# Expert products of a mixture-of-experts kernel, by whole blocks and by 2x2 blocks with seven block products

## The chip, the cores and the metric

The kernel runs on one core of a Trainium2 chip. A core has a matrix engine (TensorE, PE in the profile; its weight loads are listed as PEld), a vector engine (VectorE, DVE), a scalar engine (ScalarE, ACT), a programmable engine (GpSimd, POOL) and a sequencer that mostly issues transfers (SyncE, SP). They share an on-chip memory of 128 partitions, SBUF; TensorE writes its results to a second one, PSUM, in eight banks of 512 float32 values per partition. Each engine works through its own list of instructions in order and waits for others on semaphores. The metric is the time of the launch on the device, in microseconds, as the median of several runs; the profile shows one further execution.

## The reference

Two parts run one after the other: causal attention with a window of 64, and a layer of eight experts, of which each token uses the one with the largest router logit.

```python
# attention: q, k, v of shape (8, 8, 576, 64), window 64, softmax, times v -> x of shape (4608, 512)
logits = x @ w_gate                       # (4608, 8)
expert_idx = np.argmax(logits, axis=1)
gate_w = softmax(logits)[arange, expert_idx]
for e in range(8):                        # over the tokens of each expert
    h = np.maximum(x_sorted[lo:hi] @ w1[e], 0.0)     # 512 -> 1024
    y_sorted[lo:hi] = h @ w2[e]                      # 1024 -> 512
out = gate_w[:, None] * y
```

Everything is float32. The inputs come from a fixed seed, so the number of tokens per expert is fixed: 669, 400, 748, 505, 592, 390, 566 and 738.

## The kernel before

The kernel has three stages. The first (lines 100 to 350) computes the attention in 96 small steps that are interleaved by hand, stores the rows of x in DRAM (`x_dram`) and collects the router's logits. It also loads expert 0's weights (lines 334 to 336) into the first of the weight buffers, `ws[0]`.

The second stage (lines 353 to 479), some 40 us, routes. The tokens of each expert are laid out in slots, in tiles of TB = 128 slots that belong to one expert each; an expert's last tile is padded. VectorE computes each token's slot, and 36 matmuls with one-hot matrices (lines 473 to 477) turn that around into `perm_i`, the token in each slot, and `gate_s`, its gate. Also computed are `tile_e` (the expert of each tile), `load_i` (whether a tile must load weights: whether its expert differs from that of the tile NW before it, which used the same buffer) and `used_i` (how many tiles there are). The sizes of these operations depend on NS (slot columns), NTILE (the most tiles there can be, 43) and NCUT (the fewest, 36).

The third stage (lines 482 to 560) works through the tiles, and it is this that the change rewrites. For each tile:

- `fetch(i)` reads the expert and the load flag into registers of SP, issues the two conditional weight loads of 2 MB (w1 and w2) into buffer i % 3 on SP's queue, and has GpSimd gather the tile's 128 rows of x (`indirect_dma_start`, line 503). It runs two tiles ahead.
- `turn(i)` transposes the rows in four 128x128 blocks on TensorE (line 511); VectorE copies them to SBUF (line 512).
- `work(i)` makes the first layer in 32 matmuls, weights stationary, 128 slots streaming (line 523). In the profile a float32 matmul shows as two passes, so these are 64 entries. VectorE clears the negative values of the first half of h (line 530), ScalarE those of the second (line 528). Then comes `turn(i + 1)`, and the second layer in 8 matmuls (16 passes) with blocks of h stationary and 512 columns of w2 streaming (line 535). ScalarE multiplies by the gate (line 539), and GpSimd scatters the rows to the output (line 541).

The framework's scheduler orders each engine's list by readiness and by the order of the program, except for SP, whose order is the program's (line 489). The first 36 tiles are straight code; the rest are in pairs under `tc.If(used > i0)` (lines 555 to 560), and nothing is moved across the border of an If. With the given tokens 40 tiles are used.

Of the kernel before, what the change touches and what calls it, by code (L numbers as in the profile page):

```python
# [10 lines left out]
F32 = mybir.dt.float32  # L11
BF16 = mybir.dt.bfloat16
I32 = mybir.dt.int32
AF = mybir.ActivationFunctionType
ALU = mybir.AluOpType
AX = mybir.AxisListType
PSUM = bass.MemoryType.PSUM
# [18 lines left out]
def kernel(  # L36
# [10 lines left out]
    nc = tc.nc  # L47
    P = nc.NUM_PARTITIONS
    B, H, S, D = q.shape
    NT, DM = out.shape  # L50
    E = moe_w_gate.shape[1]
    FF = moe_w1.shape[2]
    scale = 1.0 / math.sqrt(D)

    NG = H // 2
# [5 lines left out]
    NTB = BG * S // P  # L61
    NJ = NT // P
    FT = FF // P
    TB = P
    NTILE = (NT + TB - 1) // TB + E - 1
    NS = NTILE
    NW = 3
    NCUT = (NT + TB - 1) // TB
    assert D == WINDOW and 2 * D == P and NG * P == DM and NB * WINDOW == S
    assert S - SM == WINDOW and KB == NV + 1 and NTB * P == BG * S and B % BG == 0 and NTILE * TB <= 128 * P  # L70
# [5 lines left out]
    x_dram = dram.tile([NT + 1, DM], F32, name="x_dram")  # L76
# [402 lines left out]
        V.tensor_copy(out=gate_s[:], in_=slots[:, 1, :])  # L479


    with (
        tc.tile_pool(name="wp", bufs=1) as wp,
        tc.tile_pool(name="mp", bufs=2) as mp,
        tc.tile_pool(name="xgp", bufs=1) as xgp,
        tc.tile_pool(name="ps_xt", bufs=2, space=PSUM) as ps_xt,
        tc.tile_pool(name="ps_h", bufs=4, space=PSUM) as ps_h,
        tc.tile_pool(name="ps_y", bufs=2, space=PSUM) as ps_y,
        tc.manual_schedule(engines={mybir.EngineType.SP}),
    ):  # L490
        HF = FT // 2
        NX = 4
        ws += [weights(wp, i) for i in range(1, NW)]
        xgs = [xgp.tile([P, DM], F32, name=f"xg{i}") for i in range(NX)]
        xgTs = [xgp.tile([P, NG, TB], F32, name=f"xgT{i}") for i in range(2)]

        def fetch(i):
            w1, w2 = ws[i % NW]
            e = nc.sync.value_load(tile_e[0:1, i : i + 1], min_val=0, max_val=E - 1)
            new = nc.sync.value_load(load_i[0:1, i : i + 1], min_val=0, max_val=1)  # L500
            nc.sync.dma_start(out=w1[:], in_=w1v[:, bass.ds(e, 1), :, :], cond=new, cond_hint=False)
            nc.sync.dma_start(out=w2[:], in_=w2v[:, bass.ds(e, 1), :, :], cond=new, cond_hint=False)
            nc.gpsimd.indirect_dma_start(  # L503
                out=xgs[i % NX][:], out_offset=None, in_=x_dram[:, :],
                in_offset=bass.IndirectOffsetOnAxis(ap=perm_i[:, i : i + 1], axis=0),
            )

        def turn(i):
            tp = ps_xt.tile([P, NG, P], F32, name="tp")
            for g in range(NG):  # L510
                nc.tensor.transpose(out=tp[:, g, :], in_=xgs[i % NX][:, g * P : (g + 1) * P], identity=ident[:])  # L511
            nc.vector.tensor_copy(out=xgTs[i % 2][:], in_=tp[:])  # L512

        def work(i, ahead):
            w1, w2 = ws[i % NW]
            xgT = xgTs[i % 2]
            hT = mp.tile([P, FT, TB], F32, name="hT")
            for m in range(2):
                hp = ps_h.tile([P, HF, TB], F32, name="hp")
                for f in range(HF):  # L520
                    for g in range(NG):
                        c0 = (m * HF + f) * P
                        nc.tensor.matmul(  # L523
                            hp[:, f, :], lhsT=w1[:, 0, g, c0 : c0 + P], rhs=xgT[:, g, :],
                            start=(g == 0), stop=(g == NG - 1),
                        )
                if m:
                    nc.scalar.activation(out=hT[:, m * HF :, :], in_=hp[:], func=AF.Relu)  # L528
                else:
                    nc.vector.tensor_scalar_max(hT[:, 0:HF, :], hp[:], 0.0)  # L530
            if ahead:
                turn(i + 1)
            yp = ps_y.tile([P, DM], F32, name="yp")
            for f in range(FT):
                nc.tensor.matmul(  # L535
                    yp[:], lhsT=hT[:, f, :], rhs=w2[:, 0, f, :], start=(f == 0), stop=(f == FT - 1),
                )
            y = mp.tile([P, DM], F32, name="y", bufs=4)
            nc.scalar.activation(out=y[:], in_=yp[:], func=AF.Copy, scale=gate_s[:, i : i + 1])  # L539

            nc.gpsimd.indirect_dma_start(  # L541
                out=out[:, :], out_offset=bass.IndirectOffsetOnAxis(ap=perm_i[:, i : i + 1], axis=0),
                in_=y[:], in_offset=None, bounds_check=NT - 1, oob_is_err=False,
            )

        AHEAD = NW - 1
        for i in range(AHEAD):
            fetch(i)
        turn(0)
        for i in range(NCUT):  # L550
            fetch(i + AHEAD)
            work(i, True)

        used = nc.values_load(used_i[0:1, 0:1], min_val=NCUT, max_val=NTILE)
        for i0 in range(NCUT, NTILE, 2):
            with tc.If(used > i0):
                for i in range(i0, min(i0 + 2, NTILE)):
                    if i + AHEAD < NTILE:
                        fetch(i + AHEAD)
                    work(i, i + 1 < NTILE)  # L560


# [26 lines left out]
```

## Time and profile before

| what | before |
|---|---|
| median of 3 runs | 901.77 us (900.93 to 903.26) |
| the profiled execution | 907.11 us, span 905.4 us |
| attention and its start | 0 to about 263 us |
| routing | to about 302 us |
| expert stage | 302 to 892 us, then 13 us to the end of the span |
| TensorE busy in the span | 843.1 us (93%) |
| VectorE, ScalarE, GpSimd busy | 231.6, 181.7, 124.6 us |
| weight-load issues on SP | 86, of 2 MB each, of which the flag lets some through |
| 2 KB-row gathers and scatters | 42 and 40, each about 1.0 us of GpSimd |

The profile lists the work by groups: the source line, the engine, the operation, the tiles it writes and reads, the shape and number of instances, then their busy time and mean duration, and after the bar how long the engine had stood idle before them and what ended that. Matmuls are pipelined, so their mean duration is longer than the distance from one to the next, and the distance is what costs. A view in order of time has the start, the length and the work. A view by stretches has the busy time of each engine in a window, the clock granted to TensorE as a share of its full one, and the share of the transfer engines that was in use. An arrow names what ended a wait.

### The profile page before, as it was taken

What the parts mean: (1) busy time and instruction counts of PE and PEld (TensorE: products, weight loads), DVE (VectorE), ACT (ScalarE), POOL (GpSimd) and SP (SyncE); (2) the same over time, 40 slices, a digit from 0 to 9 for tenths busy, and PEclk for the clock granted to TensorE, in tenths of its full rate; (3) what the DMA queues carried; (4) which work ended last, traced back from release to release, by engine and by line L of the source; (5) the groups of instructions that cost most, each with busy time, mean ns of one, the idle gap of its engine ahead of it and who ended that gap; (6) DMA issues with size and microseconds to landing.
All of it is one profiled execution on the core that took longest, in us unless ns stands there. A gap on an engine that the chain in (4) does not pass through costs nothing. (4 is left out here: it accounts for less than half of the span.)

```text
span 905.4 us, 16347 instructions
## 1 busy us (share of the span) xinstructions
PE 843.1 (93%) x6668; PEld 617.7 (68%) x6668; DVE 231.6 (26%) x500; ACT 181.7 (20%) x486; POOL 124.6 (14%) x177
## 2 busy tenths in 40 slices
PE   7997999998953699999999999999999999999993
PEld 5775776776733577686767777686777768677772
DVE  4664665664655000000101000010101001010100
ACT  4553554553510000001000000010000001000000
POOL 3111111011000201111111111111111111101010
PEclk9998999998985599999999999999999999999998
DMA  6668677886020661793951494891794871880110
GB/s 139 150 163 200 142 190 193 212 221 160 3 105 0 235 230 36 280 320 144 315 212 47 148 347 165 308 315 39 240 321 156 314 256 36 316 294 23 36 47 11
DMA packets 164863, 159.99 MB, mean 177 GB/s; under 512 B 118320, under 2 KB 118320, under 8 KB 164786
## 3 DMA queue, kind: packets, MB, share of 16 engines
q1 hardware_dynamic: 153362, 129.01, 45.8%
q0 software_dynamic: 6560, 20.45, 6.2%
q10 hardware_dynamic: 4864, 9.44, 3.1%
q8 instruction: 55, 0.90, 0.4%
q14 instruction: 22, 0.18, 0.1%
HBM read 219.69 MB, written 19.92 MB: 265 GB/s over the span
## 5 line engine op out<-in xcount | busy, mean ns | idle before, releaser
L523 PEld LDWEIGHTS hp<-xgT,w 128*128 128x128 f32 x2560 | 294.1, 193 | 18.8 <-issue 18.7
L523 PE MATMUL hp<-xgT,w 128*128 128x128 f32 x2560 | 294.4, 276 | 0.0
L535 PE MATMUL yp<-w,hT 128*128 128x512 f32 x640 | 281.3, 592 | 0.0
L535 PEld LDWEIGHTS yp<-w,hT 128*128 128x128 f32 x640 | 118.5, 190 | 133.9 <-issue 133.9
L530 DVE TENSOR_SCALAR hT<-hp 128x512 f32<-128x512 f32 x40 | 27.7, 692 | 390.9 <-PE hp L523 390.9
L237 ACT ACTIVATE pr<-sc,mx 128x128 f32<-128x128 f32 x288 | 79.4, 375 | 71.9 <-DVE mx L234 53.3
L528 ACT ACTIVATE hT<-hp 128x512 f32<-128x512 f32 x40 | 23.9, 597 | 310.2 <-PE hp L523 310.2
L541 POOL DMA_INDIRECT out_dram<-y,perm_i x40 | 40.6, 1016 | 316.7 <-ACT y L539 303.2
L539 ACT ACTIVATE y<-yp,gate_s 128x512 f32<-128x512 f32 x40 | 27.5, 687 | 266.1 <-PE yp L535 266.1
L503 POOL DMA_INDIRECT xg<-x_dram,perm_i x42 | 41.0, 975 | 235.6 <-PE tp L511 179.2
L512 DVE COPY xgT<-tp 128x512 f32<-128x512 f32 x41 | 28.3, 691 | 137.2 <-PE tp L511 137.2
L234 DVE TENSOR_REDUCE mx<-sc 128x3 f32<-128x384 f32 x96 | 49.1, 553 | 42.5 <-PE sc L227 41.1
L246 PE MATMUL tr<-ident,pr 128*128 128x128 f32 x288 | 49.5, 287 | 0.1
L246 PEld LDWEIGHTS tr<-ident,pr 128*128 128x128 f32 x288 | 34.7, 146 | 20.1 <-ACT qT L190 7.7
L227 PE MATMUL sc<-kT,qT 64*64 64x128 f32 x1152 | 47.7, 289 | 0.1
L227 PEld LDWEIGHTS sc<-kT,qT 64*64 64x64 f32 x1152 | 34.3, 139 | 13.0 <-issue 8.3
L261 PE MATMUL px<-va,pT 128*64 128x65 f32 x640 | 43.1, 231 | 0.0
L168 POOL COPY vb<-va 64x520 f32<-64x520 f32 x32 | 19.7, 617 | 158.5 <-DMA va<-in_v_dram 144.4
L261 PE MATMUL px<-vb,pT 128*64 128x65 f32 x512 | 41.4, 229 | 0.0
L307 PE MATMUL lg<-xT,wg 128*32 128x384 f32 x96 | 39.9, 498 | 0.7 <-DVE xT L287 0.7
L261 PEld LDWEIGHTS px<-vb,pT 128*64 128x64 f32 x512 | 33.4, 141 | 8.8 <-DVE xT L287 4.0
L261 PEld LDWEIGHTS px<-va,pT 128*64 128x64 f32 x640 | 36.3, 138 | 2.9 <-issue 2.8
(93 smaller groups left out, 476.6 us busy)
## 6 DMA issues: line engine op xcount, KB each, us to landing
w<-in_moe_w_dram SPq DMA_DIRECT2D x86, 2048.0 KB
qs<-in_q_dram SPq DMA_DIRECT2D x64, 128.0 KB
ks<-in_k_dram SPq DMA_DIRECT2D x64, 128.0 KB
va<-in_v_dram SPq DMA_DIRECT2D x64, 128.0 KB
x_dram<-xs ACTq DMA_DIRECT2D x8, 1024.0 KB
qs<-in_q_dram SPq DMA_DIRECT2D x32, 32.0 KB
ks<-in_k_dram SPq DMA_DIRECT2D x32, 32.0 KB
vb<-in_v_dram SPq DMA_DIRECT2D x32, 32.0 KB
```

Of the source, the lines that this page charges most:

```text
L227: nc.tensor.matmul(out_, lhsT=qT[rows, t, a * WINDOW : (a + 1) * WINDOW], rhs=rhs, start=False, stop=True, skip_group_check=True,)
L234: nc.vector.tensor_reduce(out=mx[:], in_=scs[h][:], axis=AX.X, op=ALU.max, negate=True)
L237: nc.scalar.activation(out=pr[:, m, :], in_=scs[h][:, m, :], func=AF.Exp, bias=mx[:, m : m + 1])
L246: nc.tensor.transpose(out=tr[:, m, :], in_=prs[h][:, m, :], identity=ident[:])
L261: nc.tensor.matmul(px[a * D : (a + 1) * D, h, m, :], lhsT=pTs[h][:, m, a * D : (a + 1) * D], rhs=vt[:, h, :], start=True, stop=True, skip_ ...
L307: nc.tensor.matmul(lgs[bg][c * WC : (c + 1) * WC, :], lhsT=wg[:, g, :], rhs=xTs[u][:, c, :], start=(g == 0), stop=(g == NG - 1), skip_grou ...
L503: nc.gpsimd.indirect_dma_start(out=xgs[i % NX][:], out_offset=None, in_=x_dram[:, :], in_offset=bass.IndirectOffsetOnAxis(ap=perm_i[:, i : ...
L512: nc.vector.tensor_copy(out=xgTs[i % 2][:], in_=tp[:])
L523: nc.tensor.matmul(hp[:, f, :], lhsT=w1[:, 0, g, c0 : c0 + P], rhs=xgT[:, g, :], start=(g == 0), stop=(g == NG - 1),)
L530: nc.vector.tensor_scalar_max(hT[:, 0:HF, :], hp[:], 0.0)
L535: nc.tensor.matmul(yp[:], lhsT=hT[:, f, :], rhs=w2[:, 0, f, :], start=(f == 0), stop=(f == FT - 1),)
L541: nc.gpsimd.indirect_dma_start(out=out[:, :], out_offset=bass.IndirectOffsetOnAxis(ap=perm_i[:, i : i + 1], axis=0), in_=y[:], in_offset=N ...
```

## The change

Tiles hold 256 slots, as two halves of 128. There are two weight buffers for three. Each layer's product is cut in 2x2 blocks: the first layer's weights in halves of the 512 inputs and halves of the 1024 outputs, with the tile's two halves of slots; the second layer's product in the two halves of slots, halves of 1024 and halves of 512. Seven products of blocks replace eight, in the form of Strassen's method by Winograd, with sums of blocks made beforehand and results combined afterwards.

- Sums of weight blocks: `sums_w1` on GpSimd, four of 1024 elements per partition for each tile; `sums_w2` on VectorE, the same size.
- Sums of the transposed tokens: four of 256 on GpSimd, after ScalarE has copied the transposes to SBUF.
- Sums of the hidden blocks: four of 512 on VectorE.
- First layer (`hidden`): seven products of eight 128x128x128 matmuls each. Two products add into one PSUM bank where the method wants their sum, with another product between them while ScalarE or VectorE reads the first. VectorE makes five combinations, ScalarE a copy and four ReLUs.
- Second layer (`output`): seven products of four matmuls with 256 streaming columns. The gates are applied as the products leave PSUM, three times on ScalarE and five times, with an addition, on VectorE. Two scatters follow.
- Order (`step`): the first layer of tile i, the transposes of tile i+1, then the second layer of tile i-1. Gathers run two tiles ahead, w1 two tiles, w2 one.
- After 18 tiles of straight code each further step is inside an If that holds the next one; the Else of each holds the second layer of the tile before it. 25 tiles are the most there can be.

```diff
-    TB = P
+    TB = 2 * P
+    C = TB // P
-    NS = NTILE
-    NW = 3
+    NS = NTILE * C
+    NW = 2
...
+        xgs = [[mp.tile([P, DM], F32, name=f"xg{i}_{c}") for c in range(C)] for i in range(2)]
+        xq = mp.tile([P, 2, 2, HG, P], F32, name="xq")
+        xs = mp.tile([P, 4, HG, P], F32, name="xs")
+        hqs = [mp.tile([P, 2, 2, HF, P], F32, name=f"hq{i}") for i in range(2)]
+        hs = mp.tile([P, 4, HF, P], F32, name="hs")
...
+        tps = [ps_xt.tile([P, NG, P], F32, name=f"tp{i}") for i in range(2)]
+        hps = [ps_h.tile([P, HF, P], F32, name=f"hp{i}") for i in range(3)]
+        yps = [ps_y.tile([P, HM], F32, name=f"yp{i}") for i in range(3)]
+        def left_sums(eng, s, a11, a12, a21, a22):
+            eng.tensor_tensor(out=s[:, 0], in0=a21, in1=a22, op=ALU.add)
+            eng.tensor_tensor(out=s[:, 1], in0=s[:, 0], in1=a11, op=ALU.subtract)
+            eng.tensor_tensor(out=s[:, 2], in0=a11, in1=a21, op=ALU.subtract)
+            eng.tensor_tensor(out=s[:, 3], in0=a12, in1=s[:, 1], op=ALU.subtract)
+        def right_sums(eng, t, b11, b12, b21, b22):
+            eng.tensor_tensor(out=t[:, 0], in0=b12, in1=b11, op=ALU.subtract)
+            eng.tensor_tensor(out=t[:, 1], in0=b22, in1=t[:, 0], op=ALU.subtract)
+            eng.tensor_tensor(out=t[:, 2], in0=b22, in1=b12, op=ALU.subtract)
+            eng.tensor_tensor(out=t[:, 3], in0=t[:, 1], in1=b21, op=ALU.subtract)
...
         def turn(i):
+            for c in range(C):
+                tp = tps[c]
+                for g in range(NG):
+                    nc.tensor.transpose(
+                        out=tp[:, g, :], in_=xgs[i % 2][c][:, g * P : (g + 1) * P], identity=ident[:]
+                    )
+                nc.scalar.copy(out=xq[:, :, c], in_=tp[:].rearrange("p (a g) s -> p a g s", a=2))
+            right_sums(nc.gpsimd, xs, xq[:, 0, 0], xq[:, 0, 1], xq[:, 1, 0], xq[:, 1, 1])
...
+        def hidden(i):
+            a11, a12, a21, a22 = w1q(i)
+            s, hq = sums[i % NW][0], hqs[i % 2]
+            def product(acc, a, b, first=True):
+                for f in range(HF):
+                    for g in range(HG):
                         nc.tensor.matmul(
+                            acc[:, f, :], lhsT=a[:, g, f * P : (f + 1) * P], rhs=b[:, g, :],
+                            start=(first and f == 0 and g == 0), stop=(g == HG - 1), skip_group_check=True,
                         )
+            relu = partial(nc.scalar.activation, func=AF.Relu)
+            p1, u2, u3 = part
+            x, y = bank(hps, 0), bank(hps, 0)
+            product(x, a11, xq[:, 0, 0])
+            nc.scalar.copy(out=p1[:], in_=x[:])
+            product(y, s[:, 1], xs[:, 1])
+            V.tensor_tensor(out=u2[:], in0=y[:], in1=p1[:], op=ALU.add)
+            product(x, a12, xq[:, 1, 0], False)
+            relu(out=hq[:, 0, 0], in_=x[:])
+            product(y, s[:, 2], xs[:, 2], False)
+            V.tensor_tensor(out=u3[:], in0=y[:], in1=p1[:], op=ALU.add)
+            z, w = bank(hps, 0), bank(hps, 0)
+            product(z, s[:, 0], xs[:, 0])
+            V.tensor_tensor(out=hq[:, 1, 1], in0=z[:], in1=u3[:], op=ALU.add)
+            relu(out=hq[:, 1, 1], in_=hq[:, 1, 1])
+            product(w, a22, xs[:, 3])
+            V.tensor_tensor(out=hq[:, 1, 0], in0=u3[:], in1=w[:], op=ALU.subtract)
+            relu(out=hq[:, 1, 0], in_=hq[:, 1, 0])
+            product(z, s[:, 3], xq[:, 1, 1], False)
+            V.tensor_tensor(out=hq[:, 0, 1], in0=z[:], in1=u2[:], op=ALU.add)
+            relu(out=hq[:, 0, 1], in_=hq[:, 0, 1])
+        def output(i):
+            b11, b12, b21, b22 = w2q(i)
+            t, hq, y2 = sums[i % NW][1], hqs[i % 2], ys[i % 2]
+            a11, a12, a21, a22 = hq[:, 0, 0], hq[:, 1, 0], hq[:, 0, 1], hq[:, 1, 1]
+            left_sums(V, hs, a11, a12, a21, a22)
...
+            product(x, a11, b11)
+            scaled(out=p1a[:], in_=x[:], scale=gates[0])
+            scaled(out=p1b[:], in_=x[:], scale=gates[1])
+            product(y, hs[:, 1], t[:, 1])
+            onto(u2[:], y[:], 0, p1a[:])
+            product(x, a12, b21, False)
+            scaled(out=y2[0][:, lo], in_=x[:], scale=gates[0])
+            product(y, hs[:, 2], t[:, 2], False)
+            onto(u3[:], y[:], 1, p1b[:])
+            z, w = bank(yps, 1), bank(yps, 1)
+            product(z, hs[:, 0], t[:, 0])
+            onto(y2[1][:, hi], z[:], 1, u3[:])
+            product(w, a22, t[:, 3])
...
+            product(z, hs[:, 3], b22, False)
+            onto(y2[0][:, hi], z[:], 0, u2[:])
...
+        def sums_w1(i):
+            left_sums(nc.gpsimd, sums[i % NW][0], *w1q(i))
+        def sums_w2(i):
+            right_sums(V, sums[i % NW][1], *w2q(i))
+        def step(i):
+            hidden(i)
+            if i + 1 < NTILE:
                 turn(i + 1)
+            if i + 2 < NTILE:
+                gather(i + 2)
+                load_w(i + 2, 0)
+            if i + 1 < NTILE:
+                sums_w1(i + 1)
+            if i:
+                output(i - 1)
+                if i + 1 < NTILE:
+                    load_w(i + 1, 1)
+            sums_w2(i)
+        gather(0)
+        load_w(0, 0)
+        load_w(0, 1)
+        gather(1)
+        load_w(1, 0)
+        load_w(1, 1)
+        sums_w1(0)
+        turn(0)
         for i in range(NCUT):
+            step(i)
...
+            with tc.If(used > i) as there:
+                step(i)
+                more(i + 1)
+            taken[:] = was
+            with there.Else():
+                output(i - 1)
+        more(NCUT)
```

## The prediction, made before the result was known

> **What bounds the kernel now.** I read the page's groups first, then busy time by stretches, then the order of time of two tiles late in the expert stage, then the start of that stage. The profiled execution took 907.11 us (span 905.4 and 1.7 around it); the median is 901.77, so it runs 5.3 us long, and my differences are carried over to the median.
>
> Busy time in stretches (stretch, its length, then PE, weight load, VectorE, ScalarE, GpSimd, granted clock, DMA share, GB/s):
>
> ```profile
> 271.00:312.00 41.00, 17.65 (x81) 16.98 (x81) 15.04 (x25) 0.00 (x0) 4.62 (x5) 0.50 0.23 84
> 312.00:892.00 580.00, 579.76 (x3357) 426.35 (x3356) 55.32 (x80) 50.88 (x80) 75.97 (x77) 1.00 0.56 196
> ```
>
> In the expert stage TensorE is never free: 579.8 of 580 us at full clock, the others at 10 to 13%. Whatever shortens TensorE's list there shortens the kernel, until another engine is late. One tile in order of time (start, length, what):
>
> ```profile
> 841.38 7.03 PE L535 MATMUL yp<-w,hT 128*128 128x512 f32 x16
> ...
> 848.25 7.31 PE L523 MATMUL hp<-xgT,w 128*128 128x128 f32 x64
> 848.25 7.11 PEld L523 LDWEIGHTS hp<-xgT,w 128*128 128x128 f32 x63 [0.24 <-issue]
> ...
> 855.39 0.60 PE L511 MATMUL tp<-ident,xg 128*128 128x128 f32 x4
> ...
> 855.83 7.03 PE L535 MATMUL yp<-w,hT 128*128 128x512 f32 x16
> ```
>
> Starts are what counts: the second layer holds TensorE for 848.25-841.38 = 6.87 us (429 ns per 512 columns), the first for 855.39-848.25 = 7.14 (111.6 ns per 128), the transposes 0.44 (110 each): 14.45 us a tile. Weight loads run at the same 111.6 ns and hide. The 40 tiles make 578 us.
>
> The groups that price the new work (instances, total, mean ns):
>
> ```profile
> L530 DVE TENSOR_SCALAR hT<-hp 128x512 f32<-128x512 f32 x40 | 27.7, 692 | 390.9 <-PE hp L523 390.9
> L528 ACT ACTIVATE hT<-hp 128x512 f32<-128x512 f32 x40 | 23.9, 597 | 310.2 <-PE hp L523 310.2
> L539 ACT ACTIVATE y<-yp,gate_s 128x512 f32<-128x512 f32 x40 | 27.5, 687 | 266.1 <-PE yp L535 266.1
> L168 POOL COPY vb<-va 64x520 f32<-64x520 f32 x32 | 19.7, 617 | 158.5 <-DMA va<-in_v_dram 144.4
> L270 DVE TENSOR_TENSOR xs<-px,rec 128x384 f32<-128x384 f32 x48 | 26.7, 556 | 1.4
> L172 POOL COPY vb<-va 64x390 f32<-64x390 f32 x32 | 16.2, 507 | 22.3 <-DMA va<-in_v_dram 11.9 <-PE sc L227 8.7
> L471 DVE TENSOR_TENSOR hi<-hi,tok_m 128x1548 f32<-128x1548 f32 x1 | 1.8, 1772 | 0.0
> L397 DVE TENSOR_TENSOR oh<-logits,r_mx 128x288 f32<-128x288 f32 x1 | 0.5, 460 | 0.0
> ```
>
> The start of the stage, in order of time: gathers are issued one per 1.26 us, and the first lands some 7 us later.
>
> ```profile
> 302.22 1.14 POOL L503 DMA_INDIRECT xg<-x_dram,perm_i  x1 [42.28 <-DVE gate_s L479]
> ...
> 306.18 0.95 POOL L503 DMA_INDIRECT xg<-x_dram,perm_i  x1 [0.30 <-issue]
> ...
> 311.93 9.41 PE L523 MATMUL hp<-xgT,w 128*128 128x128 f32 x64
> ```
>
> **How many tiles.** The reference's seeded inputs send 669, 400, 748, 505, 592, 390, 566 and 738 tokens to the eight experts. In tiles of 128 that is 6+4+6+4+5+4+5+6 = 40, as the x40 says; in tiles of 256 it is 3+2+3+2+3+2+3+3 = 21, which hold 42 old ones. Padding eats 5% of the 12.5% that seven products for eight save.
>
> **TensorE per new tile.** First layer: 7 products of 8 matmuls in two passes, 112 x 111.6 ns = 12.50 us. Second: 7 of 4 in two passes over 256 columns, a width that no row has. Between 128 (111.6) and 512 (429) lies 217.5 on the line; half the 512 is 214.6, twice the 128 is 223.2. I take the line, as both rows lie on it: 56 x 217.5 = 12.18. Transposes 8 x 0.11 = 0.88. Sum 25.56; 21 tiles 536.8 against 578: **-41.2 us** (-44.6 to -34.5). The one transpose group of a tile that is never used exists in both.
>
> **VectorE per tile.** From L397 and L471 an operation on two SBUF inputs costs 0.16 us + 1.04 ns an element: four weight sums of 1024 at 1.22 = 4.9, four sums of hidden blocks of 512 at 0.69 = 2.8. Five combinations of 512 out of PSUM at 0.69 (L530, L270) = 3.5, five of 256 at 0.42 = 2.1. Together 13.3 of 25.6 us. **ScalarE:** two transposed copies, one copy of a product and four ReLUs make seven passes of 512 at 0.60 (L528) = 4.2, three scalings of 256 lie between L237's 375 ns for 128 and L539's 687 for 512, 0.48 each: 5.6. Both fit beside TensorE.
>
> **GpSimd per tile.** Four sums of 1024 and four of 256 on two inputs, two gathers, two scatters. No row has a two-input operation of GpSimd. L168 and L172 give a copy 0.18 us + 0.85 ns an element: 1.04 us for 1024, 0.39 for 256. Lower end: a second input is free; upper end: it costs a second copy, 2.09 and 0.79. I take the upper, since two streams must be read. 4 x 2.09 + 4 x 0.79 + 4 x 1.0 (L503, L541) = 15.5 us, at least 9.7; both under 25.6. A scatter queued behind a sum goes up to 2.09 late, and its buffer is wanted again only two tiles on. The Trainium skill, "GPSIMD Engine Reference", Performance versus the Vector engine, gives 4497 ns for a two-input add of 2048, 2.2 ns an element; by it GpSimd would have an estimated 16.7 us a tile, the same verdict.
>
> **The waits inside a tile.** TensorE now comes back to a PSUM bank that another engine must have read, with one other product between: 1.79 us in the first layer, 1.74 in the second. The handover costs about 0.26 us (the first half ends at 848.25+3.57 = 851.82, VectorE starts at 852.08), the release 0.14 (in the attention stage a VectorE copy ends at 225.73 and the waiting weight load starts at 225.87). So the first layer's two waits for VectorE have 1.79-0.26-0.69-0.14 = 0.70 us to spare, the second's two 0.92, those for ScalarE 0.44 or more (two scalings of 0.48 in 1.74). They hold only while VectorE is free: a weight sum of 1.22 just begun eats 0.5 too much. Queued behind a late combination on VectorE are the next combinations and the hidden sums, which only the following tile's output needs. With VectorE's other work at 7.7 of 25.6 us, four waits x 0.3 chance x about 0.25 = 0.3 us a tile, **+6.3** in all (0 to +15). The interleaving hides the rest: a hidden block has a whole layer (12 us) until its product, the transposed tokens pass ScalarE and GpSimd (about 5 us) while the other tile's output holds TensorE.
>
> **The head.** GpSimd is in order: gathers until 307.1, four sums of expert 0's weights until 315.5, then two token sums until 317.1. The first product starts as before at 311.9 and, at the slow start's 147 ns (9.41/64), ends at 314.3; the second waits until 317.2: +2.9 (0 if a sum costs 1.04; +8.4 if the scheduler puts the weight sums ahead of the gathers, which wait for the slot table). Tile 0 has no output between its first layer and tile 1's: copies and two token sums show, +1.0. Three routing operations grow from 1548 to 1800 elements (+0.26 each), four shrink (-0.15 each): +0.2. Slot matmuls of 100 for 86 columns are held by their 128-column load. Sum **+4.1** (0.2 to 9.6).
>
> **The tail.** Two scatters follow the last combination for one: +1.0. The last output lies in an Else block: VectorE sums its hidden blocks only after the previous output's last combination, 0.26+0.42+1.38+0.14 = 2.2 against 1.74 of cover: +0.5. The jump: existing Ifs show no gap on TensorE, so 0 at best; if each engine must fetch its code, I bound it by the fastest DMA landing in the trace, 3.4. I take 2. Sum **+3.5** (1 to 5).
>
> **DMA.** Weight loads fall from 23 pairs to 15 (a change of expert reloads two buffers, not three). SP's list stays in order of need: layer 1's load of tile i+2 waits for first layer i, then layer 2's of i+1 for output i-1. A 2 MB half at the page's best slice, 348 GB/s, takes 6 us and has over 20 before its sums. Nothing; it would cost only if slower than 100 GB/s.
>
> **Sum.** 907.1-41.2+6.3+4.1+3.5 = 879.8 profiled; minus 5.3 is **874.5, say 875**. Own range 860 to 893.
>
> **Rivals.** (1) *VectorE and GpSimd block each other*, slower. Nothing in the trace shows both on SBUF sums together: GpSimd's rows in the expert stage are DMA issues alone, so a loss of 0 is as open as a whole one. If a VectorE sum must wait out a GpSimd sum of 2.09, its eight fillers grow from 7.7 to some 16 us, and a combination behind one can come up to 2.09+1.22-0.7 = 2.6 late. Four waits x 0.63 x about 1.0 = 2.5 us a tile, 53 in all in place of 6.3: 921. It decides above (27.3+6.3)/21 = 1.6 us a tile. The Trainium skill speaks against the change here: "SBUF — State Buffer", Who interferes with whom, says a VectorE instruction with two SBUF inputs contends with a GpSimd instruction that reads SBUF, and that the second to issue "fully blocks". By it the sum is an estimated 921, without it 875; no run here shows it yet. Against it: list scheduling can place the sums away from the waits, as gathers are already issued tiles early.
> (2) *GpSimd becomes the bound*: needs 25.6-5.4 us over 5120 elements, 3.9 ns an element, 4.7 times its copy. At 28 us a tile: +50, 925.
> (3) *Every product start costs an issue gap.* The attention stage shows 0.17 us of "issue" before loads that had waited; here 14 starts x 0.17 x 21 = +50, 918. Against it: three hand-offs a tile show none today. At the four tight waits alone it is +14, 889.
>
> **How the numbers follow.** My case 0.60, (1) 0.24, (2) 0.06, (3) 0.10. The measurement can tell about 0.3% (2.7 us). Faster: nearly all of mine, a fifth of (1), half of (3): 0.66; same 0.05; slower 0.29. The range to hold it 8 times in 10 runs from 860 to 922, into the middle of (1).
>
> **What would show it.** Right: x2352 first-layer and x1176 second-layer matmuls, starts 111.6 and about 217 apart, a tile every 26 us, TensorE 98% busy. Wrong: VectorE sums well above 0.69 and 1.22 or GpSimd's above 2.1 while the other runs (1); GpSimd without idle (2); TensorE holes of 0.17 at each product (3). My forecast falls if 256 columns cost over 230 ns or a tile loses over 1.6 us.

## The result and the profile after

The changed kernel takes 1053.36 us (median of 4 runs, 1042.62 to 1061.36) against 902.51 (900.93 to 905.41) for the kernel before on the same chip. Two of the changed kernel's runs, 1058.53 and 1061.36, were in a slower state, so the ratio and all differences below take the other two, 1045.4 us in the mean. That is 1.158 times as long, with an interval of 1.150 to 1.165. The prediction of 875 us, faster, was wrong in sign, and the time lies far above its range. Two things make up the loss, and either alone is enough for a kernel slower than before: VectorE's list was put in an order in which it stands waiting for a weight load with TensorE's next work queued behind it, and VectorE's sums were held up by GpSimd's. With both taken away the same seven products run in 861.82 us, 0.953 times the time before.

The profiled execution took 1042.62 us (span 1040.9). Busy time by stretches of the expert stage, with the same columns as before (start and end, length, then PE, weight load, VectorE, ScalarE, GpSimd, granted clock, DMA share, GB/s):

```profile
306.00:1028.00 722.00, 580.62 (x3695) 542.95 (x3693) 327.76 (x375) 112.56 (x211) 383.39 (x256) 0.90 0.32 111
```

Before, TensorE was busy for 579.8 of 580 us at clock 1.00. Now it stands idle for 722.0-580.6 = 141 us, and its busy time has not come down to the 537 us that the prediction worked out, because the mean granted clock is 0.90. Here is what ended TensorE's waits in that stretch (waiting line, releasing line, total us, times, longest):

```profile
PE hp L573 <- DVE part L584: 118.6, 16, 9.4
PE yp L609 <- DVE y L617: 9.4, 4, 2.9
PE hp L573 <- POOL xs L523: 6.8, 2, 3.5
PE hp L573 <- DVE hq L591: 3.7, 3, 1.2
```

One wait makes 118.6 of the 141 us. Line 584 is the first layer's first combination (`u2 = y + p1`); until VectorE has read that bank, the product of block a12's sum cannot be added into it. VectorE itself takes 0.69 us for it, so the question is what VectorE does before. One tile in order of time, first TensorE:

```profile
629.09 1.95 PE L573 MATMUL hp<-xq,w 128*128 128x128 f32 x16
630.88 1.95 PE L573 MATMUL hp<-xs,s 128*128 128x128 f32 x16
632.66 1.95 PE L573 MATMUL hp<-xq,w 128*128 128x128 f32 x16
642.40 6.59 PE L573 MATMUL hp<-xs,s 128*128 128x128 f32 x32 [7.79 <-DVE part L584]
648.83 1.95 PE L573 MATMUL hp<-xs,w 128*128 128x128 f32 x16
```

and then VectorE:

```profile
629.69 0.68 DVE L518 TENSOR_TENSOR hs<-hq,hs 128x512 f32<-128x512 f32 x1
639.39 1.23 DVE L522 TENSOR_TENSOR s<-w 128x1024 f32<-128x1024 f32 x1 [9.01 <-DMA w<-in_moe_w_dram]
640.53 1.22 DVE L524 TENSOR_TENSOR s<-w 128x1024 f32<-128x1024 f32 x1
641.66 0.69 DVE L584 TENSOR_TENSOR part<-hp,part 128x512 f32<-128x512 f32 x1
```

The product that line 584 reads ends at 632.7. By then the first sum of the w2 blocks (line 522) is ahead of it in VectorE's list. In the program these sums stand at the end of a step, behind all combinations; the scheduler moved two of them forward. Their weights are loaded into a buffer that the output just ahead of this first layer frees (there are two buffers, so it is the output of the tile two before), and SP issues that load at 629.28, when the output ends (this row merges two issues, and the first one is meant):

```profile
629.28 21.70 SPq L538 DMA_DIRECT2D w<-in_moe_w_dram  x2
```

So VectorE stands idle for 9.01 us, makes two sums, and reads the bank 9 us late. The load takes 639.39-629.28 = 10.1 us from issue to first use; in the 14 waits of this kind behind the stage's first one it is 9.5 to 10.7.

The hole has a second price. The two products after it need 648.83-642.40 = 6.43 us for 32 passes, where products without a hole before them start 1.78 us apart, so that 32 passes take 3.57. The granted clock is 1.00 from 629.1 to 632.6, 0.50 from 642.4 to 645.6, and 1.00 again from 648.8. Behind the 15 holes of 6.4 to 9.4 us in the first layer the next 32 passes take 5.0 to 6.5 us, some 33 us more in all; that is most of the 44 us by which TensorE is busy for longer than the 537 of the prediction.

The groups show the rest (instances, total, mean ns):

```profile
L522 DVE TENSOR_TENSOR s<-w 128x1024 f32<-128x1024 f32 x21 | 36.3, 1731 | 132.3 <-DMA w<-in_moe_w_dram 132.3
L515 POOL TENSOR_TENSOR s<-w 128x1024 f32<-128x1024 f32 x22 | 52.1, 2368 | 228.1 <-DMA w<-in_moe_w_dram 191.3
L517 POOL TENSOR_TENSOR s<-w 128x1024 f32<-128x1024 f32 x22 | 56.6, 2572 | 0.0
```

VectorE's sum waited 132.3 us for its weights, GpSimd's 191.3 for its own, which delays only GpSimd. And VectorE's sum takes 1731 ns in the mean where the one above took 1.23 us. What holds it shows elsewhere in order of time:

```profile
839.44 5.37 DVE L517 TENSOR_TENSOR hs<-hq 128x512 f32<-128x512 f32 x1
839.60 2.35 POOL L517 TENSOR_TENSOR s<-w 128x1024 f32<-128x1024 f32 x1
841.91 2.34 POOL L518 TENSOR_TENSOR s<-w,s 128x1024 f32<-128x1024 f32 x1
844.73 0.47 DVE L617 SCALAR_TENSOR_TENSOR y<-yp,gate_s,party 128x256 f32<-128x256 f32 x1
845.25 2.91 PE L609 MATMUL yp<-w,hs 128*128 128x256 f32 x8 [2.87 <-DVE y L617]
```

A sum of hidden blocks that takes 0.68 us elsewhere lasts 5.37 us, until GpSimd has ended the sum that it was at and the two behind it. The combination behind it is late and TensorE waits 2.87 us. So this profile holds the predicted rival (1) too, though only 9.4 us of waits are put down to it. How much it costs when the order is right, the profile can't tell; the experiments can.

### The profile page after: what moved, and what is told of

Read it like the earlier page. It is cut to its first block, busy times and chain, and to the rows that moved or that the text cites. A ratio compares the mean times of both kernels' runs of the same rounds, so it can differ in the third digit from the quotient of the medians.

```text
span 1040.9 us, 17516 instructions
## 1 busy us (share of the span) xinstructions
PE 838.9 (81%) x7008; PEld 729.6 (70%) x7008; DVE 509.3 (49%) x798; ACT 244.2 (23%) x618; POOL 440.6 (42%) x359
## 5 line engine op out<-in xcount | busy, mean ns | idle before, releaser
L573 PE MATMUL hp<-xs,s 128*128 128x128 f32 x1008 | 154.8, 324 | 125.5 <-DVE part L584 118.6
L573 PEld LDWEIGHTS hp<-xs,s 128*128 128x128 f32 x1008 | 149.3, 238 | 129.0 <-DVE part L584 121.7
L515 POOL TENSOR_TENSOR s<-w 128x1024 f32<-128x1024 f32 x22 | 52.1, 2368 | 228.1 <-DMA w<-in_moe_w_dram 191.3
L609 PE MATMUL yp<-s,hs 128*128 128x256 f32 x504 | 115.7, 379 | 0.0
L609 PEld LDWEIGHTS yp<-s,hs 128*128 128x128 f32 x504 | 95.7, 190 | 13.2 <-DVE hs L516 0.2
L522 DVE TENSOR_TENSOR s<-w 128x1024 f32<-128x1024 f32 x21 | 36.3, 1731 | 132.3 <-DMA w<-in_moe_w_dram 132.3
L573 PE MATMUL hp<-xq,w 128*128 128x128 f32 x672 | 85.6, 283 | 0.0
L573 PEld LDWEIGHTS hp<-xq,w 128*128 128x128 f32 x672 | 83.9, 200 | 1.5 <-ACT xq L557 0.3
L609 PE MATMUL yp<-w,hq 128*128 128x256 f32 x336 | 79.7, 379 | 0.8 <-issue 0.8
L609 PEld LDWEIGHTS yp<-w,hq 128*128 128x128 f32 x336 | 62.1, 190 | 8.7 <-issue 1.2
L517 POOL TENSOR_TENSOR s<-w 128x1024 f32<-128x1024 f32 x22 | 56.6, 2572 | 0.0
L516 POOL TENSOR_TENSOR s<-s,w 128x1024 f32<-128x1024 f32 x22 | 54.8, 2490 | 0.0
```

Source lines behind the costliest of these rows:

```text
L515: eng.tensor_tensor(out=s[:, 0], in0=a21, in1=a22, op=ALU.add)
L516: eng.tensor_tensor(out=s[:, 1], in0=s[:, 0], in1=a11, op=ALU.subtract)
L517: eng.tensor_tensor(out=s[:, 2], in0=a11, in1=a21, op=ALU.subtract)
L522: eng.tensor_tensor(out=t[:, 0], in0=b12, in1=b11, op=ALU.subtract)
L573: nc.tensor.matmul(acc[:, f, :], lhsT=a[:, g, f * P : (f + 1) * P], rhs=b[:, g, :], start=(first and f == 0 and g == 0), stop=(g == HG - 1 ...
L609: nc.tensor.matmul(acc[:], lhsT=a[:, f, :], rhs=b[:, f, :], start=(first and f == 0), stop=(f == HF - 1), skip_group_check=True,)
```

## The experiments

Each ratio is to the kernel before on the same chip, where it took 903.1 to 904.8 us; differences in us between runs on different chips carry that spread.

The theory after the profile: *the order of VectorE's list* costs most of the time (a sum that waits for a load ahead of a combination that is due). The rival: *GpSimd's sums hold VectorE's*, and are the reason that it runs late.

**No weight loads from the third tile on.** The load flag is cleared, so nothing waits for a transfer; the sums stay and read old weights.

```diff
-        V.tensor_tensor(out=load_i[:, NW:], in0=te[:, NW:], in1=te[:, 0 : NTILE - NW], op=ALU.not_equal)
+        V.memset(load_i[:, NW:], 0)
```

> The changed kernel with every engine's list the same, but the load flag set to zero from the third tile on, so that the 14 later pairs of weight loads are skipped at run time (this leaves out the weights of all experts but the first). Queue theory: VectorE's list has the first sum of the second layer's weight blocks, which waits for a transfer, ahead of the first combination of the next first layer, and TensorE stands behind it 16 times for 118.6 us and then runs on a slowed clock for some 40 us more; without transfers both go: about 885 us (870 to 910). Port theory: VectorE's and GpSimd's sums in SBUF block each other; all of them still run, so the time stays above 1000 us.

Measured: 946.26 us, 1.047 [1.041, 1.052] of before. It is neither. The wait for line 584 is gone, but another one has come up:

```profile
PE yp L609 <- DVE y L617: 46.2, 16, 3.3
```

In order of time it is the picture seen once above, now in nearly every tile:

```profile
652.69 5.35 DVE L517 TENSOR_TENSOR hs<-hq 128x512 f32<-128x512 f32 x1
652.84 2.34 POOL L517 TENSOR_TENSOR s<-w 128x1024 f32<-128x1024 f32 x1
655.15 2.33 POOL L518 TENSOR_TENSOR s<-w,s 128x1024 f32<-128x1024 f32 x1
```

I read it so: while VectorE waited for loads, GpSimd did much of its summing without it, and once the loads no longer hold them apart, they meet.

**No first-layer weight sums on GpSimd from the third tile on.**

```diff
-            if i + 1 < NTILE:
+            if i + 1 < NW:
                 sums_w1(i + 1)
```

> The changed kernel without GpSimd's sums of the first layer's weight blocks from the third tile on (this leaves out those sums; the products read old ones). Queue theory: the transfers and VectorE's list stay, so the 16 waits behind the weight sum stay; only the small waits that follow a lengthened VectorE sum go (9.4 us at one line, 3.7 at another, 6.8 behind token sums): 1010 to 1040 us. Port theory: 9.4 of GpSimd's 12.5 us of sums a tile are gone, so most of the loss goes: under 930 us.

Measured: 1018.76 us, 1.127 [1.121, 1.133]. VectorE's sums are short again (line 517 at 682 ns in the mean, line 524 at 1217), and the wait for line 584 is still 114.0 us in 15 waits. So the order of the list does it in this kernel, with no help from GpSimd's weight sums.

**Both edits together.**

> The changed kernel with both removals at once: the later weight loads skipped at run time and GpSimd's weight sums only for the first two tiles (this leaves out the other experts' weights and those sums). If the wait on the transfers and the blocking between VectorE and GpSimd are the whole loss, TensorE runs at 25.6 us a tile as in the run with all sums on VectorE: 860 to 875 us. If a third cause holds it, such as the order of VectorE's list by itself or gaps at product starts, above 890 us.

Measured: 875.47 us, 0.968 [0.965, 0.972], at the upper end of what was expected. Against the changed kernel, the loads alone give 99 us, GpSimd's weight sums alone 27, both together 170. Each hides behind the other, and a kernel without either is faster than before. It does not do the whole work, though; the next runs do.

**VectorE's list in the order of the program.** The framework is told to leave VectorE alone, as it was for SP.

```diff
-        tc.manual_schedule(engines={mybir.EngineType.SP}),
+        tc.manual_schedule(engines={mybir.EngineType.SP, mybir.EngineType.DVE}),
```

> The changed kernel with one edit: VectorE's list is kept in the order of the program, so that the sums of the second layer's weight blocks stand behind the combinations of the output before them, where their transfer landed long ago. Queue theory: no wait on a transfer before a combination any more; instead the four sums (4.9 us) stand ahead of the next tile's first combination, which is 1.1 us too late a tile if nothing lengthens them: 900 to 920 us; if GpSimd's sums double them, 4 to 5 us a tile, 960 to 990. Port theory alone: no change, above 1020 us.

Measured: 1016.13 us, 1.124 [1.120, 1.130], which I had not allowed for. No wait of VectorE for a load is left in the stage. But the w2 sums, now together at the end of a step, fall beside GpSimd's sums: the first of the four takes more than three times its length, the second 2.37 us for 1.22. The next tile's first combination is behind them. From the groups:

```profile
L522 DVE TENSOR_TENSOR s<-w 128x1024 f32<-128x1024 f32 x21 | 86.2, 4103 | 0.0
```

and from TensorE's waits:

```profile
PE hp L573 <- DVE part L584: 84.3, 16, 7.3
```

The same wait at line 584 has another cause here, which is why its name alone decides nothing.

**All sums on VectorE, in an order written by hand.** VectorE keeps the program's order. The sums of hidden blocks now stand ahead of the next first layer; the others come as lists of single instructions and are placed singly or in small groups behind those combinations that leave VectorE free: the first layer's for the next tile behind u2, u3 and the next combination of `hidden`, the second layer's behind the first layer and behind u2 and u3 of `output`, by when the load has landed.

```diff
-        tc.manual_schedule(engines={mybir.EngineType.SP}),
+        tc.manual_schedule(engines={mybir.EngineType.SP, mybir.EngineType.DVE}),
...
+        WE, XE = V, V
...
+            run(*right_sums(XE, xs, xq[:, 0, 0], xq[:, 0, 1], xq[:, 1, 0], xq[:, 1, 1]))
...
             V.tensor_tensor(out=u2[:], in0=y[:], in1=p1[:], op=ALU.add)
+            run(*fill[0:2])
...
             V.tensor_tensor(out=u3[:], in0=y[:], in1=p1[:], op=ALU.add)
+            run(*fill[2:3])
...
+            return left_sums(WE, sums[i % NW][0], *w1q(i))
...
+            if i:
+                hidden_sums(i - 1)
+            hidden(i, sums_w1(i + 1) if later and WE is V else ())
+            w2s = sums_w2(i)
+            if later:
+                turn(i + 1, w2s)
...
+                output(i - 1, w2s[1:])
```

> All sums on VectorE (none on GpSimd), VectorE's list in the order of the program, and the sums placed where a combination is not due: hidden sums of the last tile ahead of the first layer, weight sums two behind one combination and one behind others, each behind the landing of its transfer. VectorE then has 20 us of 25.6 a tile. Queue theory with the port as the second loss: both gone, 21 tiles at 25.6 to 26.5 us: 865 to 890 us, faster than the kernel before. If neither is the cause, or if 78% is too full for VectorE with its order fixed, above 920 us.

Measured: **861.82 us (859.79 to 862.5), 0.953 [0.949, 0.956]**: faster than both kernels, by 43.0 us against the one before on its chip (904.84) and by some 184 against the changed one, and a little below the 865 to 890 expected. It computes everything. The stage by stretches, as above:

```profile
306.00:848.00 542.00, 537.04 (x3694) 505.08 (x3693) 399.72 (x550) 112.43 (x211) 112.87 (x82) 1.00 0.43 149
```

VectorE is busy for 400 of 542 us, 72 more than in the changed kernel, yet TensorE is idle for only 5 us, at full clock. The 180 us between 722 and 542 are 136 of idle time and 44 of busy time at the slower clock. A tile now takes 25.47 us, from one start of the first product to the next (of the timeline):

```profile
601.09 1.95 PE L583 MATMUL hp<-xq,w 128*128 128x128 f32 x16
626.56 1.95 PE L583 MATMUL hp<-xq,w 128*128 128x128 f32 x16
```

**The same, with the first layer's weight sums back on GpSimd.** This prices GpSimd alone, with the order right.

```diff
-        WE, XE = V, V
+        WE, XE = nc.gpsimd, V
```

> The kernel with all sums on VectorE and its order by hand, but the four sums of the first layer's weight blocks given back to GpSimd. VectorE has 15 us of work a tile instead of 20, and no sum ahead of its transfer, so that only the blocking between the two engines differs. If it is what the profile of the changed kernel suggests (VectorE sums of 0.68 and 1.22 us growing to 4 and more beside GpSimd's 2.35): 920 to 1000 us. If the blocking only fills idle time: 855 to 870 us, as before or better by the relief.

Measured: 998.1 us, 1.105 [1.102, 1.108]. Moving four sums a tile off VectorE costs 136 us. In order of time:

```profile
614.53 2.37 POOL L518 TENSOR_TENSOR s<-s,w 128x1024 f32<-128x1024 f32 x1
615.30 6.75 DVE L517 TENSOR_TENSOR hs<-hq 128x512 f32<-128x512 f32 x1
616.85 2.35 POOL L519 TENSOR_TENSOR s<-w 128x1024 f32<-128x1024 f32 x1
619.16 2.34 POOL L520 TENSOR_TENSOR s<-w,s 128x1024 f32<-128x1024 f32 x1
623.90 0.68 DVE L594 TENSOR_TENSOR part<-hp,part 128x512 f32<-128x512 f32 x1
```

VectorE's sum waits not only for the sum that GpSimd is at, but for that one and the two behind it. GpSimd's own take 2.35 us, as alone. The combinations, which read PSUM and one input in SBUF, keep their 0.68 to 0.69 us, also the 19 of the first layer that run beside a GpSimd sum.

**The changed kernel with all sums on VectorE, the order left to the scheduler.** This prices the order alone.

```diff
-            right_sums(nc.gpsimd, xs, xq[:, 0, 0], xq[:, 0, 1], xq[:, 1, 0], xq[:, 1, 1])
+            right_sums(V, xs, xq[:, 0, 0], xq[:, 0, 1], xq[:, 1, 0], xq[:, 1, 1])
...
-            left_sums(nc.gpsimd, sums[i % NW][0], *w1q(i))
+            left_sums(V, sums[i % NW][0], *w1q(i))
```

> The changed kernel with GpSimd's sums given to VectorE and the order left to the scheduler: no blocking, VectorE at 78% of a tile. Queue theory: the scheduler again puts sums of the second layer's weight blocks ahead of their transfers, now ahead of the second combination, which is due 7.4 us after the layer's start while the transfer lands some 10 us after it: 2 to 5 us in each of about 15 tiles and a slowed clock after them: 890 to 950 us. If the blocking was the whole loss: 860 to 875 us.

Measured: 1105.14 us, 1.223 [1.220, 1.226], the slowest of all, against an expected 890 to 950. I had thought that the scheduler would do better with GpSimd out of the way. Instead both layers' sums are now ahead of combinations, and the wait for w1's load, harmless on GpSimd, is on VectorE too. TensorE's waits in the expert stage:

```profile
PE hp L573 <- DVE part L584: 99.2, 15, 8.6
PE yp L609 <- DVE party L617: 77.2, 12, 7.2
```

and VectorE's own:

```profile
DVE s L522 <- DMA w<-in_moe_w_dram: 113.3, 14, 9.9
DVE s L515 <- DMA w<-in_moe_w_dram: 83.5, 14, 7.3
```

With these the four corners are measured, in us:

| | first-layer weight sums on GpSimd (in the scheduler's and the program's order also the sums of tokens) | all sums on VectorE |
|---|---|---|
| order by the scheduler | 1045 | 1105 |
| VectorE's order fixed | 998 (by hand), 1016 (program) | 862 |

No single repair helps much: the scheduler's order costs 243 us when VectorE has all sums, and GpSimd's sums cost 136 when the order is right.

**What of GpSimd's work holds VectorE?** Two variants of the hand-ordered kernel with the weight sums on GpSimd, in which from the third tile on each of these sums is replaced by two fills (which only write) or by two copies (which read one input and write); the sums themselves are left out.

```diff
+            return [partial(lambda k: nc.gpsimd.memset(s[:, k], 0.0), k) for k in range(4) for _ in range(2)]
```

```diff
+            return [partial(lambda k: nc.gpsimd.tensor_copy(out=s[:, k], in_=a[k]), k) for k in range(4) for _ in range(2)]
```

> The kernel with the order by hand and GpSimd's weight sums, in which GpSimd from the third tile on does two fills with zero in place of each sum (this leaves out those sums; it writes 1024 elements twice and reads none). If what holds VectorE's sums is GpSimd's reading of SBUF, they stay at 0.68 and 1.22 us and the time is that of all sums on VectorE or a little less, 855 to 870 us. If any long GpSimd instruction that uses SBUF holds them, 950 to 1000 us.

> The same with two copies in place of each sum (this leaves out those sums; one input read per instruction). By the row of GpSimd's copies in the kernel before a copy of 1024 takes about 1.04 us, so eight take 8.3 us where the four sums take 9.4. If reading SBUF is what counts, VectorE's sums grow as beside the sums: 940 to 1000 us. If only the second input of a GpSimd sum takes what VectorE's second input needs: 855 to 880 us.

Measured: fills 860.78 us, 0.953 [0.950, 0.955]; copies 949.28, 1.051 [1.049, 1.053]. The groups with fills:

```profile
L673 POOL MEMSET s<- 128x1024 f32 x160 | 149.3, 964 | 5.9 <-PE hp L583 3.0
L530 DVE TENSOR_TENSOR s<-w 128x1024 f32<-128x1024 f32 x21 | 25.5, 1216 | 0.0
```

and with copies:

```profile
L673 POOL COPY s<-w 128x1024 f32<-128x1024 f32 x160 | 174.8, 1133 | 149.3 <-DMA w<-in_moe_w_dram 148.2
L530 DVE TENSOR_TENSOR s<-w 128x1024 f32<-128x1024 f32 x21 | 46.1, 2197 | 0.0
```

Both kinds keep GpSimd busy for a like time, 149 and 175 us. But the two kinds don't fall at the same times: the copies wait 148.2 us for loads, the fills for none, and no fill meets a sum of line 517, so the kernel's time alone would not show the cause. The sums of the w2 blocks do meet fills. In order of time, with fills:

```profile
617.55 0.98 POOL L673 MEMSET s<- 128x1024 f32 x1
618.19 1.22 DVE L531 TENSOR_TENSOR s<-w,s 128x1024 f32<-128x1024 f32 x1
```

Of the 84 sums of w2 blocks 43 run beside a fill, for 34.7 us in all, and none takes over 1.23 us. Beside copies 25 of the 84 run, for 62.5 us, with a mean of 3.06 us and a longest of 8.32. So it is GpSimd's reading of SBUF that holds a VectorE instruction with two SBUF inputs.

This is what the Trainium skill says in "SBUF — State Buffer", section Who interferes with whom: such an instruction contends with a GpSimd instruction that reads SBUF, and not with one that only writes it. In its closing summary the page has the second one to issue blocked until the first finishes; the runs show more than that, 6.75 us beside three sums in a row (the run with the hand order and GpSimd's weight sums).

**The kernel before, with whole pairs of tiles.** Every expert gets an even number of the old tiles, 42 in all as in the changed kernel, to price the padding by itself.

```diff
-    NTILE = (NT + TB - 1) // TB + E - 1
+    NTILE = (NT + TB - 1) // TB + 2 * (E - 1)
...
-        cuts = iota([P, NCUT], [[TB, NCUT]])
+        cuts = iota([P, NCUT], [[2 * TB, NCUT]])
...
+        V.tensor_scalar_mul(nt[:], nt[:], 2.0)
```

> The kernel before with one difference: each expert's slots are rounded up to 256 instead of 128, so that 42 tiles of 128 are worked through instead of 40. It prices the padding that tiles of 256 bring, without the seven products. By the prediction's working two tiles at 14.45 us: +29 us, about 931. If empty slots cost less, or the loads change the order, within 10 us of the kernel before.

Measured: 934.99 us, 1.035 [1.033, 1.036]; +31.9 us, for two tiles of 14.45 = 28.9. In the profiles the time from the first product's start to the last one's end grows by 29.0 us, from 579.7 to 608.6, which is the two tiles; the first product starts 7.9 us earlier, and the tail behind the last one is 7.2 longer. In the hand-ordered kernel that stretch takes 540.0 us. So seven products for eight, with what else the change brings, are worth 68.6 us there, of which the padding takes back over four tenths.

## Why the prediction was wrong, and where it was right

**The step that failed** is the one that costs the transfers at nothing: "SP's list stays in order of need ... A 2 MB half at the page's best slice, 348 GB/s, takes 6 us and has over 20 before its sums. Nothing; it would cost only if slower than 100 GB/s." SP's list was in order. But the 20 us take VectorE's list to be in the program's order, where the w2 sums come last in a step, though line 489 of the kernel before (491 of the changed one) fixes SP's order only. The scheduler had two of them ahead of the combination of line 584, and from the load's issue at 629.28 to the end of that combination's product at 632.7 there are 3.4 us, not over 20. Its duration was wrong as well: 10.1 us where I took 6 from the best slice of the page. That is some 207 GB/s, twice the 100 below which it was to cost anything. With a load of 6 us the two sums would end at 637.7 by the same times, so the holes would be smaller and not gone. In place of nothing the runs show 118.6 us of idle time at that wait and some 33 of slower passes behind its holes; with all sums on VectorE the scheduler's order costs 243 us (1105 against 862).

**Rival (1)** was right in its mechanism and is shown by the fills and the copies, but its size and its place in the argument were off. It was priced at 53 us, with a VectorE sum waiting out one GpSimd sum of 2.09; measured by itself it costs 136 us, 6.5 a tile. VectorE often waits out two or three in a row, and TensorE's passes slow down behind the holes: in that run's stage TensorE is idle for 94 us and busy for 43 longer, at a clock of 0.92. Against it I said that "list scheduling can place the sums away from the waits". The scheduler did the opposite: it put VectorE's sums ahead of the combinations, and that was the larger loss. The forecast was on the wrong side since each of the two alone exceeds what the products save. The 861.82 us of the hand-ordered kernel lie in the range, but they don't bear the forecast out: it is another kernel, with no sum on GpSimd.

**TensorE, -41.2 us**: right where TensorE does not wait. The starts are 111.9 ns per pass of 128 columns ((630.88-629.09)/16) and 216 per pass of 256, for 111.6 and 217.5. In the hand-ordered kernel 21 tiles of 25.47 us make 534.9, 43.1 less than the 578 before.

**The waits inside a tile, +6.3**: for the kernel that I had in mind no run bears it out; in the program's order, with GpSimd's sums, it took 1016 us. In the hand-ordered one TensorE's idle time in the whole stage is 5 us, with VectorE at 400 of 542 us, so one bank's turn between two products of 1.8 us does leave enough time. The changed kernel has 141. Two sums of the working are off, with no effect on the forecast: by its own terms two scalings on ScalarE leave 0.38 us, not 0.44, and the estimate of 16.7 us for GpSimd comes out only with 0.18 us added for each of the eight sums; by 2.2 ns an element alone it is 15.2.

**The durations**: GpSimd's sums take 2.35 and 0.73 us (2.09 and 0.79 predicted), VectorE's 1.22 and 0.68 when undisturbed (1.22 and 0.69), VectorE's combinations of the second layer 0.48 (0.42). GpSimd was busy for 383 of 722 us, so rival (2) did not come about.

**Rival (3)**, an issue gap at each product's start: no. Products without a wait start 1.79 us apart, which is 16 passes and nothing more.

**The head, +4.1**: the two waits for the sums of tokens were 3.33 and 3.49 us for 2.9 and 1.0. In the hand-ordered kernel there are none, and its first product starts at 305.27 instead of 311.93. Of these 6.7 us some 4.6 come from the slot matmuls in the routing, whose pace I had called unchanged (see the last section); and the routing's first matmuls start 2.8 us earlier in this execution, behind an attention stage that the change leaves alone.

**The tail, +3.5**: 3.8 in the hand-ordered kernel. From the last product's end to the span's end it takes 14.8 us for 13.8 before, and the last output, behind a jump, has holes of 1.15 us before its first product and 1.64 before its second. In order of time:

```profile
828.56 1.89 PE L625 MATMUL yp<-w,hs 128*128 128x256 f32 x8
831.44 1.97 PE L625 MATMUL yp<-w,hq 128*128 128x256 f32 x8 [0.99 <-issue]
834.81 2.86 PE L625 MATMUL yp<-s,hs 128*128 128x256 f32 x12 [1.41 <-DVE hs L518]
```

Of what was to show the prediction right or wrong, the counts (x2352 and x1176) and the spacing held, and the sign for rival (1) came, with VectorE's sums far above 0.69 and 1.22 us. TensorE was to be 98% busy; it was busy for 581 of 722 us in the changed kernel and for 537 of 542 in the hand-ordered one. "A tile every 26 us" holds in the changed kernel only where no hole falls into it (26.98 us from one group of transposes at 871.13 to the next, a wait of 1.25 in it).

## What to carry to other kernels

In a list that is worked through in order, a filler that depends on a transfer must stand behind the work that another engine waits for; here the scheduler moved such fillers ahead of work that was due. So fix that engine's order by hand, and count the cover of each load from the place that the instruction really has in the list. Don't relieve VectorE by giving GpSimd elementwise work that reads SBUF while VectorE has instructions with two SBUF inputs near a critical wait: here four sums of 1024 a tile (22 x 4 x 1.22) are 107 us of VectorE's time, which its free places hold, and on GpSimd they cost the kernel 136 us. And when a profile shows one large wait, take its cause away before pricing the rest: the second cause, at 9.4 us in this profile, was worth 136 in the kernel without the first.

## What was not expected of the hardware

- A VectorE instruction with two SBUF inputs often gets no turn between GpSimd instructions that follow each other: 6.75 us beside three sums instead of 0.68, and 6.39 instead of 1.22 beside six copies, whose seventh then took 1.92 instead of 1.04. In the other direction GpSimd's sums are held less: line 517's take 2.57 us in the mean of the changed kernel for 2.35 alone, and up to 3.34 beside a VectorE sum that had started before. Combinations of 512 with one input in PSUM and one in SBUF stayed at 0.68 to 0.69 us in all these kernels, beside GpSimd's sums too. That GpSimd keeps the access from one instruction to the next is read from these durations; why it does was not tried.
- A hole of 8 us in TensorE's list makes the passes behind it slower as well: 32 in 6.43 us instead of 3.57, at a granted clock of 0.50 for the first 3.2 us. Over the stage the granted clock is 0.90, and the slower passes are 44 of the 180 us lost.
- The routing's 72 passes of slot matmuls take 15.66 us with 86 columns (217 ns each) and only 10.6 to 11.1 with 100, in the changed kernel, the hand-ordered one and the even-tiled kernel before alike. The clock makes the difference, not the pace of a width: at a granted clock of 0.50 a pass takes 213 ns at either width, and at 1.00 it takes 111 with 100 columns. In the profile of the kernel before the clock stays at 0.50 through all 72 passes; in the three others it rises to 1.00 within the first 7 us. Why it stayed low, by the width, by the moment at which they start or by chance, was not tested and stays open.
- A conditional load of 2 MB took 10.1 us from its issue to its first use, while the transfer engines were in use for 0.65 of the time; 9.5 to 10.7 us in the 14 waits counted above.
